# Joining the two Gram jobs of a unit into one job over two PSUM banks, for the last element of a DeltaNet + Mixer kernel

## The chip, the cores and the metric

The kernel runs on one core of a Trainium2 chip. The metric is the device time of one execution in microseconds (us), the median of several runs. The core's engines each work through an own queue in order: PE (TensorE, matmuls; PEld are its weight loads), DVE (VectorE), ACT (ScalarE), POOL (GpSimd), and SP, which only issues DMAs here. SBUF is the working memory, PSUM the memory that matmuls write, in banks of 512 float32 numbers per partition.

## The reference

Two blocks follow one another. The first is a delta rule over 768 steps for 4 batch elements and 8 heads with 48 features each; the second is an MLP-Mixer on the result, seen as 4 x 768 x 384.

```python
k_n = k / (norm(k) + 1e-6)
for t in range(S):                       # per batch element and head
    y[t]  = q[t] @ state
    v_old = k_n[t] @ state
    state = state + beta[t] * outer(k_n[t], v[t] - v_old)
x = y as (B, S, H*D)
u = x + (relu(x^T @ w_tok1) @ w_tok2)^T
out = u + relu(u @ w_ch1) @ w_ch2
```

## The kernel before, in words

The 768 steps of an element are cut into 6 *units* of 128 steps, so there are 24 units, numbered 0 to 23; units 18 to 23 belong to the last element. A unit has two *chunks* of 64 steps (`cc` 0 and 1). Within a chunk the delta rule is solved by matrices: products of all keys with all keys and queries (the *Grams*), the inverse of a triangular matrix made from them, and a short recurrence that takes the state from chunk to chunk.

All work is cut into named jobs, Python generators that issue a few instructions per step. A long text, `order`, says step by step which job goes on; instructions stand on each engine's queue in that order. The jobs that matter here, with the number of the unit (or of the chunk, for `r`) behind the letter:

- `c` and `d` (`grams`, L446): the Grams of chunk 0 and of chunk 1. Four steps, one for each pair of heads, issue two matmuls each (L452); the fifth is one DVE multiplication of the bank with the scaled mask `mb`, into `gm` (L455). Each job holds one of the two PSUM banks of the pool `prep`, which the `j` jobs use too.
- `p` (`prep`): norms and scales of a unit. Steps 1 and 2 are an ACT square (L476) and a DVE sum (L479), step 3 two ACT functions, step 4 a DVE reciprocal and a DVE product (L488, L489), steps 5 and 7 DVE transposes of keys and queries (L369), step 6 makes `mb` on POOL (L511), a buffer that exists once.
- `r` (`recur`): the recurrence of one chunk. Steps 1 to 4 are the matmuls `p_k` (L857), a pair of heads each; step 5 `rest` on DVE (L864); step 6 the matmuls `p_y` and `p_w` (L877, L881); step 7 the copy `w_t` on ACT (L887); step 8 the matmuls `p_s` and `p_y` (L895, L896); step 9 the new state `s_t` on DVE (L904); step 10 the copies of `y` on ACT (L909). Every step needs the one before.
- `j` (`join`): parts of the inverse. Its second step fills both `prep` banks and its third empties them with eight ACT copies (L799, L802).
- `m` (`mixer`): the Mixer of one element, its matmuls 128 rows by 128 columns; it fills the time beside the recurrence of the next element.

The small matmuls use a quarter of TensorE's 128 x 128 array each: rows 0 to 63 or 64 to 127 (the partitions of the operands), and columns 0 to 63 or 64 to 127 (the partitions of the output). Written (rows, columns) with 0 and 1 for the halves, chunk 0's Grams use the quarters (0,0) and (1,1), chunk 1's use (0,1) and (1,0). `p_k` uses (0,0) and (1,1) in a chunk 0 and (0,1) and (1,0) in a chunk 1. Step 6 and step 8 of `r` use all four. The pair of lines that says so for the Grams:

```python
p_g[PAR[i ^ cc], p]        # out: the half i ^ cc of the columns
kqt[f, p, cc]              # in: f is the half i of the rows
```

Of the kernel before, what the change touches and what calls it, by code (L numbers as in the profile page):

```python
# [10 lines left out]
ALU = mybir.AluOpType  # L11
ACTF = mybir.ActivationFunctionType

C = 64
# [9 lines left out]
def kernel(  # L24
# [39 lines left out]
    nc = tc.nc  # L64

    B, H, S, D = q.shape
# [5 lines left out]
    NP = H // 2  # L72
# [22 lines left out]
    def ps_prep(shape, name):  # L95
        return psum.tile(shape, FP32, name=name, tag="prep", bufs=2)
# [36 lines left out]
    TU = 12  # L133
# [15 lines left out]
    for kept, shape in ((kpad, [H, DP]), (qpad, [H, DP]), (kst_of, [NP, 2, D])):  # L149
        for _ in range(NL, NK):  # L150
            n = H * shape[-1]
# [13 lines left out]
    GW = D + 2 * C  # L165
# [20 lines left out]
    PAR = (slice(0, C), slice(C, 2 * C))  # L186
    FEATS = [slice(r.start, r.start + D) for r in PAR]
# [25 lines left out]
    def place(u):  # L213
        return NV + u if u < 2 else (u - 2) % NV

    def before_in(u):
        return max([x for x in range(u) if place(x) == place(u)], default=None)
# [98 lines left out]
    while rounds[-1][-1] < NU - 1:  # L316
        u = rounds[-1][-1] + 1
# [14 lines left out]
    walked = set()  # L332
# [42 lines left out]
    def load_kq(u):  # L375
        b, c = divmod(u, NCH)
        kst = kst_of[slot(u)]
        if u >= TU:
            yield from load_rows(u, 0, k)
            assert last_in(u) in ranked  # L380
            for n, _ in enumerate(stacked(kst, k, u)):
                if n == 3:
                    keys_in.add(u)
                yield
            yield from load_rows(u, 1, q)
            return
        for pad, src in ((kpad, k), (qpad, q)):
            assert last_in(u) is None or (pad is kpad, last_in(u)) in turned
            nc.sync.dma_start(
                out=pad[slot(u)][:, :, 0:D],  # L390
                in_=src[b, :, c * U : (c + 1) * U, :].rearrange("h t d -> t h d"),
            )
            pads_in.add((pad is kpad, u))
            yield
            if src is k and u >= RU:
                for n, _ in enumerate(stacked(kst, k, u)):
                    if n == 3:
                        keys_in.add(u)
                    yield

        heads = kpad[slot(u)].rearrange("t (p par) d -> t p par d", par=2)
        for cc in range(2 if u < RU else 0):
            for par in range(2):
                nc.scalar.copy(kst[PAR[par ^ cc], :, cc], heads[PAR[cc], :, par, 0:D])
                if cc and par:
                    keys_in.add(u)
                yield
# [25 lines left out]
    def blocks(t):  # L433

        if len(t.shape) == 2:
            t = t.rearrange("s (b n) -> s b n", b=NB)
        return t.rearrange("s (p c) n -> s p c n", c=2)

    def gm_of(u):
        return gms[place(u)]  # L440

    grown = set()
    grammed = set()
    made = {}

    def grams(u, cc):  # L446
        kqt = kqts[place(u)]
        p_g = ps_prep([128, NP, 2, C], "p_g")
        for p in range(NP):
            for i in range(2):  # L450
                f = PAR[i] if u < TU else FEATS[i]
                nc.tensor.matmul(p_g[PAR[i ^ cc], p], kqt[f, p, cc, 0], kqt[f, p, cc])  # L452
            yield
        assert before_in(u) is None or 2 * before_in(u) + cc in walked
        nc.vector.tensor_tensor(  # L455
            out=blocks(gm_of(u))[:, :, cc, D:GW].rearrange(
                "s p (two n) -> s p two n", two=2
            ),
            in0=p_g,
            in1=made[u][:, :, cc, None, :].to_broadcast([128, NP, 2, C]), op=ALU.mult,  # L460
        )
        grammed.add((u, cc, False))
        yield

    def prep(u):

# [84 lines left out]
    def z_of(u):  # L551
# [9 lines left out]
        out=low16,  # L561
# [6 lines left out]
        out=even,  # L568
# [5 lines left out]
        out=odd, in0=even, scalar1=-1.0, scalar2=1.0, op0=ALU.mult, op1=ALU.add  # L574
    )
    sides = const.tile([128, 2], FP32, name="sides")
    for i, side in enumerate((even, odd)):
        nc.vector.tensor_tensor(
            out=sides[:, i : i + 1], in0=low16, in1=side, op=ALU.mult
# [25 lines left out]
    def to_parts(u):  # L605
        assert grammed.issuperset([(u, 0, False), (u, 1, False)])
        rnd, j = round_of[u]
        if u < NCH:
            t = turned_of(rnd)
            both = t[:, :, j * NB : j * NB + NB].rearrange("s t b -> s b t")  # L610
            nc.scalar.copy(both, gm_of(u)[:, :, TC.start : TC.start + HB])
            yield
            _, (b1, at1, _), _, (b3, at3, _) = quarters(u)
            nc.vector.tensor_copy(out=t[at1].rearrange("s t b -> s b t"), in_=b1)
            yield
            nc.gpsimd.tensor_copy(out=t[at3].rearrange("s t b -> s b t"), in_=b3)
            masked.add(u)
            yield
            return
        if rnd not in xins:  # L620
            xins[rnd] = dram.tile([RU * 4 * NB, HB, HB], FP32, name="n_dram")
        for i, (block, _, rows) in enumerate(quarters(u)):
            nc.sync.dma_start(out=xins[rnd][rows].rearrange("b s t -> s b t"), in_=block)
            if i == 3:
                masked.add(u)
            yield
# [573 lines left out]
    jobs = {}  # L1200
    for u in range(NU):
        jobs[f"k{u}"] = load_kq(u)
        jobs[f"p{u}"] = prep(u)
        jobs[f"c{u}"], jobs[f"d{u}"] = (grams(u, cc) for cc in range(2))
        jobs[f"t{u}"] = to_parts(u)
        if u < NCH:
            jobs[f"h{u}"] = join_16(u)
        jobs[f"f{u}"] = from_parts(u)
        jobs[f"j{u}"] = join(u)
        jobs[f"v{u}"] = load_v(u)  # L1210
# [64 lines left out]
    s*2 m0 i4 m0*2 i4*2 m0 i4*5 v12*4 m0*2 j13 i4*2 m0 i4 r23 j13 m0 r24 k18*3  # L1275
    r24*3 j13 v13*2 r24 i4 r24*2 p18 i4 p18 m0 i4 p18 m0*2 i4*2 m0 r25*3 p18 r25
    p18*2 r25 m1*3 k18*2 v14 i4 v14 r24 i4*7 k19 m1*3 i4 r25 i4*2 k19*3 v13 k19*2
    v14*2 m1 r25 v13 i4*4 k19 m1 p18 m1 k19 r25*2 p18 m1*2 r26 v13 d18 r26*4 j13
    r25 m1*3 r26*2 c18*2 m1*2 r26*2 k19*4 p19*2 d18*3 c18*2 d18 f14*2 v14 r27*2
    f14*2 r27 p19*2 r27 p19 j14 r27 m1*4 s m1*2 f15*3 m1*2 c18 r26 m1*2 r27*2 j14  # L1280
    j15 j14 r27 f16 m1*3 j15*2 r27 r28*2 k20 p19*2 f16 r27 r28*2 k20*2 f16 j16 m1*4
    r28*3 f15 m1*2 s k20*2 s p19 r28 k20*3 d19 c19 k20 d19 p20 c19 t18 k20 d19*2
    p20 c19 v15 r28 p20 r29 k20*2 m1 p20 r28 c19 r29*3 v15*3 f17*2 r29 m1 p20 k21
    m1*2 c19 k21 r29*2 m1*2 d19 k21 m1*2 p20 m1*2 p20 m1*4 r29*3 m1*2 j16*2 r30
    k21*3 v16 k21*2 v15 k21 r30*4 v16 k21*2 m1 k21 m1*2 c20 r30 d20 c20*3 p21*2 c20
    r30*2 p20 d20 r30 d20*2 p21*2 d20 r31*2 r30 r31*2 t18 r31*3 p21*3 m1*2 r31*2
    c21 d21 c21 d21 c21 d21 v16 m1 v16 c21 v16 r32 d21 r32 d21 m1 t18*2 m1 r32 r31
    t19*2 r32*2 f17 m1 f17 m1*4 t19*2 c21 m1*5 p21 m1*2 f16 t20*3 j17*2 t20 t21*4
    k22 i5 k22*5 j17 k22 m1*2 k22 i5*3 r32 k22 i5*2 m1 i5 m1 r32*3 i5 k22 m1*4
    p22*2 i5 v17 p22 r33*2 k22 r33*3 p22 m1*4 p22 m1 k23 p22 i5 v20 i5*3 m1*2 r32  # L1290
    m1*4 k23 i5 k22 r33 p22 r33 v17 j17 m1*4 r33 i5 m1*6 k23 r33 k23 m1*6 k23 m1*2
    j17 v20 m1 v17*2 k23*2 m1*6 r34*2 d22 v17 k23 r34*3 m1*6 r33 i5*4 m1 r34 p23*2
    c22 d22 c22 d22 c22 d22 i5*2 r34*2 m1 r34 m1 i5*4 m1*4 v20*2 p23 r35*2 k23*3
    c22*2 r35 k23 i5*3 r35 m1*4 i5*3 m1*6 p23 m1*4 d22 t22 r34 i5 m1 p23*2 m1*4
    t22*2 r35*2 m1 f20 p23 m1 r35 m1*2 p23 f21*2 v20 f18 m1*2 v18 m1*3 t22 m1*2
    f18*3 d23 c23 d23 v18 c23 d23 m1 v18 f19*4 c23 d23 m1 c23*2 f20 r35*2 m1*5 d23
    t23*4 m1*2 j18*3 j19 f20 v18 m1 j19 m1*2 j20 i6*2 m1*4 i6*2 v18 j19 r36*5 j20
    r36 i6*2 m2 r36 r37 i6*2 r36 r37*3 m2*3 r37*2 m2 i6*8 v19*2 r37*3 m2 r38 r37
    v19 f20 v19 i6*4 f21 j21 r38 v19 r38*3 m2*3 j20 r38*2 i6*2 j21 r38*2 i6*4 m2*3
    f21 r39 r38 r39*4 m2*7 v21*2 r39*2 m2*4 j21 m2*5 r39*3 m2*2 r40*4 m2 r40*2 j21  # L1300
    i6*2 r40*2 v21 j21 m2*2 i6 v21 m2*2 i6*3 f22*3 r40*2 r41*5 f22 m2*4 r41*2 m2*7
    r41*3 m2 v21 m2*2 r42*2 j22 r42 f23 r42 j22 r42*3 m2*5 f23*2 m2*8 r42*2 j23
    m2*13 p22 m2 v22*3 j22 v22 m2*3 r43 m2 r43*2 r42 r43*2 m2 r43*2 m2*6 r43 m2 j23
    v23 r43*2 r44*4 v22 j23 r44 m2 v23*2 m2*3 r44*2 m2 r44 m2*5 r44 m2*3 r44 m2*3
    v23 r45*5 m2*8 r45 m2*2 r45 f23 j23*2 m2*2 r45*3 m2*6 r46*4 m2*2 v23 r46 m2*9
    r46*2 m2*2 r46*3 m2*7 r47*5 m2*6 r47 m2 r47 m2*2 r47 m2*6 r47 m3*6 m2*5 m3*6
    m2*11 m3*3 m2 m3*159
    """
    for word in order.split():
        name, _, n = word.partition("*")  # L1310
# [34 lines left out]
```

## Time and profile before

| | |
|---|---|
| runs | 638.39, 639.58, 640.07 us; median 639.58 us |
| the profiled execution | 637.11 us, span of its instructions 635.3 us |
| busy in the span | PE 96%, PEld 83%, DVE 70%, ACT 42%, POOL 17% |
| instructions | 21547 |
| granted TensorE clock | 0.981 of full speed on average |
| matmuls of the Grams of units 18 to 23 | first at 283.4 us, last at 385.5 us |

Busy time counts an engine's instructions without overlap. A row of the timeline has the start in us from the start of the span, the time that the row covers, engine, line, operation, tiles (output, then inputs), shapes and the number of records; in brackets stands the time for which the engine was idle before it, and what ended that. A row of a wait table has the total, the number of times, and the longest.

### The profile page before, as it was taken

To read this page: it belongs to the slowest core of one execution; us is meant where nothing else is said; L and a number is where in the kernel's file an instruction comes from. 1 tells how busy PE (TensorE), PEld (TensorE's weight loads), DVE (VectorE), ACT (ScalarE), POOL (GpSimd) and SP (SyncE) were. 2 spreads that over 40 slices of the span, in tenths; PEclk is the share of its full clock that TensorE was granted. 3 is DMA by queue.
4 is the path that set the end of the run, shared out by engine and by line. 5 is a ranking of instruction groups with operands and counts; after the bars stand their busy time and mean duration, and the time that the engine had idled before them with its cause. 6 is when DMAs were issued, how large, how long until landed. Compare 5 with 4: busy or idle time off the path is not lost.

```text
span 635.3 us, 21547 instructions
## 1 busy us (share of the span) xinstructions
PE 607.5 (96%) x9132; PEld 529.5 (83%) x9132; DVE 446.2 (70%) x1132; ACT 268.5 (42%) x693; POOL 108.2 (17%) x146
## 2 busy tenths in 40 slices
PE   8488898999999999999999999999999999999997
PEld 5367786667888888858999999769999977999997
DVE  4988877977899667987969987785627253373643
ACT  7759785447512342226624433145254230223240
POOL 2338354235310221111110010101010000000000
PEclk9979896999999999999999999999999999999999
DMA  9787566666542445154444033201020000000000
GB/s 201 129 148 166 140 134 162 170 135 157 110 115 74 82 118 110 50 125 77 95 101 103 14 95 47 66 11 37 2 54 2 27 1 0 26 1 26 2 26 26
DMA packets 135776, 50.27 MB, mean 79 GB/s; under 512 B 114656, under 2 KB 130144, under 8 KB 135680
## 3 DMA queue, kind: packets, MB, share of 16 engines
q1 hardware_dynamic: 135680, 48.89, 34.9%
q8 instruction: 72, 1.18, 0.8%
q14 instruction: 24, 0.20, 0.1%
HBM read 39.42 MB, written 9.44 MB: 77 GB/s over the span
## 4 chain that ended last, share of the span: by engine, by line
PE 78%; DVE 7%; ACT 5%; SPq 3%; DMA 3%; issue 2%; POOL 1%; ACTq 0%; POOLq 0%; DVEq 0%
PE p_o L1157 25%; PE p_r L1027 18%; PE p_c L1135 8%; PE p_h L1068 5%; PE p L1055 4%; PE p_s L895 3%; PE p_g L452 3%; PE p_k L857 3%; PE p_y L877 2%; DVE x L681 1%; DVE sub L676 1%; PE p_w L881 1%; SPq L413 1%; PE p_ut L1078 1%; DMA d<-in_moe_w_ch_dram 1%
## 5 line engine op out<-in xcount | busy, mean ns | idle before, releaser
L1157 PE MATMUL p_o<-wc,r 128*128 128x192 f32 x720 | 126.8, 330 | 0.6 <-ACT u_t L1082 0.6
L1157 PEld LDWEIGHTS p_o<-wc,r 128*128 128x128 f32 x720 | 116.6, 190 | 2.9 <-ACT u_t L1082 1.1
L1039 DVE TENSOR_TENSOR r<-r,p_r 128x512 f32<-128x512 f32 x90 | 59.7, 684 | 39.7 <-PE p_r L1027 37.2
L1086 DVE TENSOR_TENSOR xb<-xb,p_o 128x192 f32<-128x192 f32 x84 | 29.3, 350 | 58.7 <-PE p_o L1157 58.4
L1036 ACT COPY r<-p_r 128x512 f32<-128x512 f32 x54 | 31.5, 586 | 89.4 <-PE p_r L1027 88.0
L681 DVE TENSOR_TENSOR x<-x,sub 128x84 f32<-128x84 f32 (+24 forms) x178 | 59.8, 336 | 6.1
L676 DVE TENSOR_TENSOR sub<-x 128x84 f32<-128x84 f32 (+24 forms) x178 | 57.4, 322 | 6.7 <-DMA x<-n_dram 2.3
L1135 PE MATMUL p_c<-u_t,wc 128*128 128x256 f32 x216 | 51.1, 387 | 0.2 <-ACT u_t L1082 0.2
L1157 PE MATMUL p_o<-wc,s 128*128 128x192 f32 x288 | 50.1, 329 | 0.3 <-DVE xb L1086 0.3
L426 POOL TENSOR_TENSOR v_st<-v_st,nrm 128x384 f32<-128x384 f32 x24 | 20.3, 845 | 166.7 <-DMA v_st<-in_v_dram 129.1
L1157 PEld LDWEIGHTS p_o<-wc,s 128*128 128x128 f32 x288 | 46.8, 190 | 1.2 <-DVE xb L1086 0.6
L1135 PEld LDWEIGHTS p_c<-u_t,wc 128*128 128x128 f32 x216 | 39.6, 190 | 6.1 <-ACT u_t L1082 0.4
L1043 ACT ACTIVATE r<-r 128x512 f32<-128x512 f32 x54 | 33.8, 630 | 25.0 <-DVE r L1039 24.6
L452 PE MATMUL p_g<-kq 48*64 48x128 f32 (+1 forms) x704 | 38.6, 283 | 3.0 <-ACT kq L524 2.8
L511 POOL TENSOR_TENSOR mb<-mask_c,cs 128x512 f32<-128x512 f32 x20 | 21.4, 1072 | 108.0 <-DVE cs L489 40.9
L909 ACT ACTIVATE xb<-p_y 64x192 f32<-64x192 f32 x96 | 31.2, 325 | 19.6 <-PE p_y L896 12.1
L1027 PE MATMUL p_r<-u_t,wc 128*128 128x128 f32 x288 | 38.5, 277 | 0.0
L1027 PE MATMUL p_r<-t_d,wc 128*128 128x128 f32 x288 | 37.2, 280 | 0.0
L887 ACT COPY w_t<-p_w 128x192 f32<-128x192 f32 x48 | 15.3, 318 | 50.0 <-PE p_w L881 49.3
L1027 PEld LDWEIGHTS p_r<-u_t,wc 128*128 128x128 f32 x288 | 35.3, 192 | 0.3
L1055 PE MATMUL p<-xb,w 128*128 128x384 f32 x96 | 34.9, 511 | 0.0
L452 PEld LDWEIGHTS p_g<-kq 48*64 48x64 f32 (+1 forms) x704 | 28.9, 137 | 7.1 <-ACT kq L524 3.7
(184 smaller groups left out, 1216.0 us busy)
## 6 DMA issues: line engine op xcount, KB each, us to landing
d<-in_moe_w_ch_dram SPq DMA_DIRECT2D x24, 384.0 KB, 4.2
v_st<-in_v_dram SPq DMA_DIRECT2D x96, 48.0 KB, 2.7
out_dram<-xb SPq DMA_DIRECT2D x23, 192.0 KB, 1.9
kst<-in_k_dram SPq DMA_DIRECT2D x64, 48.0 KB, 2.8
n_dram<-gm SPq DMA_DIRECT2D x72, 32.0 KB, 2.0
pads<-in_k_dram SPq DMA_DIRECT2D x24, 96.0 KB, 3.1
pads<-in_q_dram SPq DMA_DIRECT2D x24, 96.0 KB, 2.5
gm<-w_dram SPq DMA_DIRECT2D x72, 32.0 KB, 2.1
```

Source lines behind the costliest of these rows:

```text
L452: nc.tensor.matmul(p_g[PAR[i ^ cc], p], kqt[f, p, cc, 0], kqt[f, p, cc])
L676: nc.vector.tensor_tensor(out=tmp, in0=y[:, :, 0:s, s : s + 1].to_broadcast([n, k, s, w]), in1=y[:, :, s : s + 1, s + 1 : m].to_broadcast( ...
L681: nc.vector.tensor_tensor(out=y[:, :, 0:s, s + 1 : m], in0=y[:, :, 0:s, s + 1 : m], in1=tmp, op=ALU.add,)
L909: nc.scalar.mul(y[:, :, D * i : D * i + D], p_y[PAR[1 - i]], 1.0 if c else -1.0)
L1027: nc.tensor.matmul(p[:, i], pieces[i // width][:, at : at + 128], f[f"u{n}"], start=first and i == 0, stop=True, skip_group_check=True,)
L1036: nc.scalar.copy(o, p)
L1039: nc.vector.tensor_tensor(out=o, in0=o, in1=p, op=ALU.add if sign > 0 else ALU.subtract)
L1043: nc.scalar.activation(o, o, ACTF.Relu)
L1055: nc.tensor.matmul(p_1[dh], piece_of(w1, c, 0)[:, dh * 128 : (dh + 1) * 128], xb[:, c], start=(c == 0), stop=(c == NCH - 1),)
L1068: nc.tensor.matmul(p_h, piece_of(w2, j, c * 128)[:, c * 128 : (c + 1) * 128], r1[j], start=(j == 0), stop=(j == NDH - 1),)
L1135: nc.tensor.matmul(p_c[:, k], piece_of(wc1, cb, f * 128)[:, f * 128 : (f + 1) * 128], u_t[:, cb], start=(cb == 0), stop=(cb == NCB - 1),)
L1157: nc.tensor.matmul(p, a[:, m], wc2[:, m, j], start=(start and i == 0), stop=(i == NM - 1), skip_group_check=True,)
```

## The change

`grams` takes a list of chunks. With one chunk it does what it did. With two it takes both `prep` banks at its first step, and each of its four matmul steps issues the four matmuls of a pair of heads, chunk 0 and chunk 1 in turn: quarters (0,0), (0,1), (1,1), (1,0). Its fifth and sixth steps are the two DVE multiplications, chunk 0 first. Units 0 to 17 keep two jobs; units 18 to 23 have the joint job, named `c`.

```diff
-    def grams(u, cc):
+    def grams(u, chunks):
         kqt = kqts[place(u)]
-        p_g = ps_prep([128, NP, 2, C], "p_g")
+        p_gs = [ps_prep([128, NP, 2, C], "p_g") for _ in chunks]
         for p in range(NP):
             for i in range(2):
-                f = PAR[i] if u < TU else FEATS[i]
-                nc.tensor.matmul(p_g[PAR[i ^ cc], p], kqt[f, p, cc, 0], kqt[f, p, cc])
+                for cc, p_g in zip(chunks, p_gs):
+                    f = PAR[i] if u < TU else FEATS[i]
+                    nc.tensor.matmul(
+                        p_g[PAR[i ^ cc], p], kqt[f, p, cc, 0], kqt[f, p, cc]
+                    )
             yield
-        assert before_in(u) is None or 2 * before_in(u) + cc in walked
-        nc.vector.tensor_tensor(
...
-        grammed.add((u, cc, False))
-        yield
+        for cc, p_g in zip(chunks, p_gs):
+            assert before_in(u) is None or 2 * before_in(u) + cc in walked
+            nc.vector.tensor_tensor(
...
+            grammed.add((u, cc, False))
+            yield
...
-        jobs[f"c{u}"], jobs[f"d{u}"] = (grams(u, cc) for cc in range(2))
+        if u < 18:
+            jobs[f"c{u}"], jobs[f"d{u}"] = (grams(u, [cc]) for cc in range(2))
+        else:
+            jobs[f"c{u}"] = grams(u, [0, 1])
```

In `order` all steps of other jobs keep their sequence. The ten steps of a `c` and `d` become six. Around them, `c20.2` being the second step of the job `c20`, the order is as follows (DMA, SP and Mixer steps that matter little here are left out):

```
unit 18 before: d18.1 r26.2-5 ... r26.6 r26.7 c18.1 c18.2 r26.8 r26.9 ... d18.2-4 c18.3 c18.4 d18.5 ... r27.1-4 ... c18.5
unit 18 after:  r26.2-5 ... r26.6 r26.7 c18.1 r26.8 r26.9 ... c18.2-4 c18.5 ... r27.1-4 ... c18.6
unit 19 before: d19.1 c19.1 d19.2 c19.2 d19.3 d19.4 c19.3 ... r29.1 ... c19.4 r29.2-4 ... c19.5 ... d19.5
unit 19 after:  c19.1 c19.2 c19.3 ... r29.1 ... c19.4 r29.2-4 ... c19.5 ... c19.6
unit 20 before: c20.1 r30.6 d20.1 c20.2-4 p21.1 p21.2 c20.5 r30.7 r30.8 d20.2 r30.9 d20.3 d20.4 p21.3 p21.4 d20.5 r31.1-4 r31.5 r31.6
unit 20 after:  r30.6 c20.1 p21.1 p21.2 r30.7 r30.8 c20.2 r30.9 c20.3 c20.4 c20.5 p21.3 p21.4 c20.6 r31.1-4 r31.5 r31.6
unit 21 before: c21.1 d21.1 c21.2 d21.2 c21.3 d21.3 ... c21.4 r32.1 d21.4 r32.2 d21.5 ... c21.5
unit 21 after:  c21.1 c21.2 c21.3 ... r32.1 c21.4 r32.2 c21.5 ... c21.6
unit 22 before: r34.1 r34.2 d22.1 r34.3 r34.4 ... r34.6 p23.1-2 c22.1 d22.2 c22.2 d22.3 c22.3 d22.4 r34.7 r34.8 ... r35.1 r35.2 c22.4 c22.5 r35.3 r35.4 ... d22.5
unit 22 after:  r34.1-4 ... r34.6 p23.1-2 c22.1-3 r34.7 r34.8 ... r35.1 r35.2 c22.4 c22.5 r35.3 r35.4 ... c22.6
unit 23 before: d23.1 c23.1 d23.2 c23.2 d23.3 ... c23.3 d23.4 ... c23.4 c23.5 r35.8 ... d23.5
unit 23 after:  c23.1 c23.2 ... c23.3 ... c23.4 c23.5 r35.8 ... c23.6
```

More of the change, by code (lines that the diff above doesn't have):

```diff
@@ L444 @@
     made = {}
-    def grams(u, cc):
+    def grams(u, chunks):
         kqt = kqts[place(u)]
-        p_g = ps_prep([128, NP, 2, C], "p_g")
+        p_gs = [ps_prep([128, NP, 2, C], "p_g") for _ in chunks]
         for p in range(NP):
             for i in range(2):
-                f = PAR[i] if u < TU else FEATS[i]
-                nc.tensor.matmul(p_g[PAR[i ^ cc], p], kqt[f, p, cc, 0], kqt[f, p, cc])
-            yield
-        assert before_in(u) is None or 2 * before_in(u) + cc in walked
[L455 to L461, printed above, removed]
-        grammed.add((u, cc, False))
-        yield
+                for cc, p_g in zip(chunks, p_gs):
[3 more added lines that the diff above has]
+                    )
+            yield
+        for cc, p_g in zip(chunks, p_gs):
+            assert before_in(u) is None or 2 * before_in(u) + cc in walked
+            nc.vector.tensor_tensor(
+                out=blocks(gm_of(u))[:, :, cc, D:GW].rearrange(
+                    "s p (two n) -> s p two n", two=2
+                ),
+                in0=p_g,
+                in1=made[u][:, :, cc, None, :].to_broadcast([128, NP, 2, C]),
+                op=ALU.mult,
+            )
+            grammed.add((u, cc, False))
+            yield
     def prep(u):
@@ L1277 @@
     p18*2 r25 m1*3 k18*2 v14 i4 v14 r24 i4*7 k19 m1*3 i4 r25 i4*2 k19*3 v13 k19*2
[L1278 to L1307, printed above, removed]
+    v14*2 m1 r25 v13 i4*4 k19 m1 p18 m1 k19 r25*2 p18 m1*2 r26 v13 r26*4 j13 r25
+    m1*3 r26*2 c18 m1*2 r26*2 k19*4 p19*2 c18*4 f14*2 v14 r27*2 f14*2 r27 p19*2 r27
+    p19 j14 r27 m1*4 s m1*2 f15*3 m1*2 c18 r26 m1*2 r27*2 j14 j15 j14 r27 f16 m1*3
@@ new lines @@
+    j15*2 r27 r28*2 k20 p19*2 f16 r27 r28*2 k20*2 f16 j16 m1*4 r28*3 f15 m1*2 s
+    k20*2 s p19 r28 k20*3 c19 k20 p20 c19 t18 k20 p20 c19 v15 r28 p20 r29 k20*2 m1
+    p20 r28 c19 r29*3 v15*3 f17*2 r29 m1 p20 k21 m1*2 c19 k21 r29*2 m1*2 c19 k21
+    m1*2 p20 m1*2 p20 m1*4 r29*3 m1*2 j16*2 r30 k21*3 v16 k21*2 v15 k21 r30*4 v16
+    k21*2 m1 k21 m1*2 r30 c20 p21*2 r30*2 p20 c20 r30 c20*3 p21*2 c20 r31*2 r30
+    r31*2 t18 r31*3 p21*3 m1*2 r31*2 c21*3 v16 m1 v16*2 r32 c21 r32 c21 m1 t18*2 m1
+    r32 r31 t19*2 r32*2 f17 m1 f17 m1*4 t19*2 c21 m1*5 p21 m1*2 f16 t20*3 j17*2 t20
@@ new lines @@
+    t21*4 k22 i5 k22*5 j17 k22 m1*2 k22 i5*3 r32 k22 i5*2 m1 i5 m1 r32*3 i5 k22
+    m1*4 p22*2 i5 v17 p22 r33*2 k22 r33*3 p22 m1*4 p22 m1 k23 p22 i5 v20 i5*3 m1*2
+    r32 m1*4 k23 i5 k22 r33 p22 r33 v17 j17 m1*4 r33 i5 m1*6 k23 r33 k23 m1*6 k23
+    m1*2 j17 v20 m1 v17*2 k23*2 m1*6 r34*2 v17 k23 r34*3 m1*6 r33 i5*4 m1 r34 p23*2
+    c22*3 i5*2 r34*2 m1 r34 m1 i5*4 m1*4 v20*2 p23 r35*2 k23*3 c22*2 r35 k23 i5*3
+    r35 m1*4 i5*3 m1*6 p23 m1*4 c22 t22 r34 i5 m1 p23*2 m1*4 t22*2 r35*2 m1 f20 p23
@@ new lines @@
+    m1 r35 m1*2 p23 f21*2 v20 f18 m1*2 v18 m1*3 t22 m1*2 f18*3 c23 v18 c23 m1 v18
+    f19*4 c23 m1 c23*2 f20 r35*2 m1*5 c23 t23*4 m1*2 j18*3 j19 f20 v18 m1 j19 m1*2
+    j20 i6*2 m1*4 i6*2 v18 j19 r36*5 j20 r36 i6*2 m2 r36 r37 i6*2 r36 r37*3 m2*3
+    r37*2 m2 i6*8 v19*2 r37*3 m2 r38 r37 v19 f20 v19 i6*4 f21 j21 r38 v19 r38*3
+    m2*3 j20 r38*2 i6*2 j21 r38*2 i6*4 m2*3 f21 r39 r38 r39*4 m2*7 v21*2 r39*2 m2*4
+    j21 m2*5 r39*3 m2*2 r40*4 m2 r40*2 j21 i6*2 r40*2 v21 j21 m2*2 i6 v21 m2*2 i6*3
@@ L1308 @@
+    f22*3 r40*2 r41*5 f22 m2*4 r41*2 m2*7 r41*3 m2 v21 m2*2 r42*2 j22 r42 f23 r42
+    j22 r42*3 m2*5 f23*2 m2*8 r42*2 j23 m2*13 p22 m2 v22*3 j22 v22 m2*3 r43 m2
+    r43*2 r42 r43*2 m2 r43*2 m2*6 r43 m2 j23 v23 r43*2 r44*4 v22 j23 r44 m2 v23*2
+    m2*3 r44*2 m2 r44 m2*5 r44 m2*3 r44 m2*3 v23 r45*5 m2*8 r45 m2*2 r45 f23 j23*2
+    m2*2 r45*3 m2*6 r46*4 m2*2 v23 r46 m2*9 r46*2 m2*2 r46*3 m2*7 r47*5 m2*6 r47 m2
+    r47 m2*2 r47 m2*6 r47 m3*6 m2*5 m3*6 m2*11 m3*3 m2 m3*159
     """
```

## The prediction

> **What bounds the kernel now.** I read the page first, then a table of stretches for the part in which the Grams of units 18 to 23 stand, then the waits of PE there, and then the timeline around each unit, engine by engine. Page, stretch (span, then busy time and records of PE, PEld, DVE, ACT, POOL) and wait:
>
> ```profile
> PE 607.5 (96%) x9132; PEld 529.5 (83%) x9132; DVE 446.2 (70%) x1132; ACT 268.5 (42%) x693; POOL 108.2 (17%) x146
> 280.00:392.00 112.00, 111.24 (x1859) 103.81 (x1859) 96.05 (x238) 46.93 (x119) 15.31 (x23) 1.00 0.38 83
> PE p_g L452 <- ACT gm L802: 0.2, 1, 0.2
> ```
>
> PE is busy in 111.24 of these 112 us. So a Gram matmul saves time if PE's next work then starts earlier, and a wait anywhere in PE's queue that nothing covers is paid in full. Shares do not answer this: overlapping matmuls all count as busy. I go by the start of the next kind of work.
>
> **How the Grams run now.** PE's timeline at units 18, 19 and 21, with the copy `w_t` of unit 18's first chunk (ACT):
>
> ```profile
> 286.62 0.62 PE L452 MATMUL p_g<-kq 48*64 48x128 f32 x8
> 287.80 0.91 PE L452 MATMUL p_g<-kq 48*64 48x128 f32 x20
> 288.47 0.63 PE L857 MATMUL p_k<-s_t,kq 48*64 48x48 f32 x16
> ...
> 301.68 1.13 PE L452 MATMUL p_g<-kq 48*64 48x128 f32 x32
> 302.57 0.62 PE L857 MATMUL p_k<-s_t,kq 48*64 48x48 f32 x16
> ...
> 320.50 1.15 PE L452 MATMUL p_g<-kq 48*64 48x128 f32 x32
> 321.42 0.62 PE L857 MATMUL p_k<-s_t,kq 48*64 48x48 f32 x16
> ```
>
> ```profile
> 286.92 0.32 ACT L887 COPY w_t<-p_w 128x192 f32<-128x192 f32 x1 [0.17 <-PE p_w L881]
> ```
>
> A unit's 16 calls show as 32 records: each call is two passes. Unit 19, where `c` and `d` alternate, takes 302.57 - 301.68 = 0.89 us for 8 passes on each of four quarters, unit 21 321.42 - 320.50 = 0.92: 0.11 us for a pass of four. Unit 18's 20 records take 288.47 - 287.80 = 0.67 us, which is d's 6 passes of 0.11; c's 4 passes run beside them. So the quarters already work side by side, one chunk beside the other, and what counts is the fullest quarter.
>
> **The change part by part.** The same 192 records and 12 DVE multiplications remain; no DMA moves, and on SP and POOL nothing is moved past anything.
>
> *Units 19, 21, 23.* Eight passes on each quarter before and after, in nearly the same places: 0. In 19 and 21 the fourth step now stands inside `p_k`, on the quarters that `p_k` uses; but those carried d's 8 passes ahead of `p_k` already, so the sum on them is unchanged. If breaking up `p_k` is not free, it is two passes, 0.22 us, for each of the two. Bounds 0 to +0.44; I take 0, as the count of passes says.
>
> *Unit 18.* `c18.1` fills the wait for `w_t`, whose copy ends at 286.92 + 0.32 = 287.24, as the old 8 records did. `c18.2-4` are 6 passes, 0.67 us, as the old 20 records. `d18.1`, which goes, stood beside a `p_k` of the other quarters, which is free, as unit 22 shows next. Sum 0, bounds -0.05 to +0.05 (the rounding of these rows).
>
> *Unit 22.* Here is PE at `c22.4`, and farther down a `p_k` with nothing in it:
>
> ```profile
> 369.66 0.26 PE L857 MATMUL p_k<-s_t,kq 48*64 48x48 f32 x2
> 369.69 0.33 PE L452 MATMUL p_g<-kq 48*64 48x128 f32 x2
> ...
> 370.26 0.60 PE L1027 MATMUL p_r<-u_t,wc 128*128 128x128 f32 x3
> ```
>
> ```profile
> 432.11 0.67 PE L857 MATMUL p_k<-s_t,kq 48*64 48x48 f32 x16
> 432.71 0.38 PE L1027 MATMUL p_r<-t_d,wc 128*128 128x128 f32 x1
> ```
>
> With the Gram step 370.26 - 369.66 = 0.60 us, without 432.71 - 432.11 = 0.60 us: the step cost nothing, since chunk 35's `p_k` is on (0,1) and (1,0) and `c22.4` was on the other two. After, `c22.4` brings chunk 1's matmuls too, on just `p_k`'s quarters: two passes of 0.11 that `p_k` must let by, and the 128-row matmuls behind it start 0.22 us later. Bounds 0 (if they slip into gaps of `p_k`) to 0.3; I take +0.22, the count of passes. `d22.1` goes from a place where it was free, and `c22.1-3` fill the same 24 records as before: 0.
>
> *Unit 20* is the one place where a DVE multiplication moves: `c20.5` stood ahead of `r30.9`, and comes now behind it. The timelines of DVE, ACT and PE:
>
> ```profile
> 316.30 0.69 DVE L455 TENSOR_TENSOR gm<-p_g,mb 128x512 f32<-128x512 f32 x1
> 316.91 0.35 DVE L904 TENSOR_TENSOR s_t<-s_t,p_s 128x192 f32<-128x192 f32 x1
> 317.17 0.20 DVE L488 RECIPROCAL ksum<-ksum 128x8 f32<-128x8 f32 x1
> 317.40 0.17 DVE L489 TENSOR_TENSOR cs<-ksum,beta_st 128x8 f32<-128x8 f32 x1
> 317.49 0.68 DVE L455 TENSOR_TENSOR gm<-p_g,mb 128x512 f32<-128x512 f32 x1
> 318.08 0.35 DVE L864 TENSOR_TENSOR rest<-p_k,v_st 128x192 f32<-128x192 f32 x1
> ```
>
> ```profile
> 315.21 0.52 ACT L476 ACTIVATE ksq<-kst 128x384 f32<-128x384 f32 x1
> 315.70 0.32 ACT L887 COPY w_t<-p_w 128x192 f32<-128x192 f32 x1
> ```
>
> ```profile
> 314.69 0.33 PE L452 MATMUL p_g<-kq 48*64 48x128 f32 x2 [0.20 <-ACT gm L802]
> ...
> 316.08 0.25 PE L896 MATMUL p_y<-w_t,gm 64*64 64x48 f32 x1
> ...
> 317.31 0.67 PE L857 MATMUL p_k<-s_t,kq 48*64 48x48 f32 x16
> 318.16 0.31 PE L877 MATMUL p_y<-s_t,kq 48*64 48x48 f32 x2 [0.19 <-issue]
> 318.49 0.25 PE L881 MATMUL p_w<-rest,gm 64*64 64x48 f32 x1
> ```
>
> First the gain that looks sure: PE idles 0.20 us ahead of `c20.1`, whose bank `j16` has not emptied; now `r30.6` goes ahead of it. But the next step, `r30.8`, starts at 316.08 because `w_t` ends at 315.70 + 0.32 = 316.02, and `w_t` starts only when the square `p21.1` (315.21 + 0.52 = 315.73) leaves ACT, which no step here changes. The 0.20 us becomes a wait for `w_t`. Gain 0, bounds -0.20 to 0.
>
> Then the loss. `rest` of chunk 31 is the last thing before `p_w` can start: it ends at 318.08 + 0.35 = 318.43, and `p_w` starts at 318.49. After the change, `c20.5` waits for all of `c20.2-4`, whose six passes stand between `p_s` and `p_k` as d's six did, so DVE starts it when it started `d20.5`: 317.49. From there the queue runs on at its old distances: the reciprocal of `p21.4` follows 318.08 - 317.49 = 0.59 us later, as `rest` did; the multiplication that follows, `c20.6`, starts 317.49 - 317.17 = 0.32 us after the reciprocal; `rest` 0.59 us after that. So `rest` starts at 317.49 + 0.59 + 0.32 + 0.59 = 318.99 instead of 318.08: +0.91 us. `s_t` of `r30.9` may come earlier, but `p_k` stays behind the six passes on its quarters, at 317.31. In PE's queue nothing but `p_k` and two `p_y` stands ahead of `p_w`: the whole 0.91 us is idle PE. Behind `rest` the two transposes of `p21`, which c21 needs, shift as well, by no more than PE itself. POOL's `mb` for unit 21 waits for `c20.6` and comes 0.91 us later, as do its readers. Bounds: 0.59 (if the reciprocal and `cs` hide) to 1.1 (if the pairs no longer overlap, about 0.09 twice more).
>
> Sum: 0 + 0 + 0.22 + 0.91 = +1.13 us; lowest -0.05 + 0 - 0.20 + 0.59 = +0.34, highest 0.44 + 0.05 + 0.3 + 1.1 = +1.9. The profiled execution took 637.11 us and would take 638.24, a factor of 1.0018. It lies 2.47 below the median of the runs shown, so I carry the difference over: 639.58 + 1.13 = 640.7 us.
>
> [...] The changed order puts matmuls of the same rows next to each other: (0,0), (0,1). Today's `p_y` and `p_w`, which read the same rows for different columns, stand so too:
>
> ```profile
> 286.50 0.22 PE L877 MATMUL p_y<-s_t,kq 48*64 48x48 f32 x1
> 286.51 0.22 PE L881 MATMUL p_w<-rest,gm 64*64 64x48 f32 x1
> 286.51 0.22 PE L877 MATMUL p_y<-s_t,kq 48*64 48x48 f32 x1
> 286.52 0.22 PE L881 MATMUL p_w<-rest,gm 64*64 64x48 f32 x1
> 286.56 0.22 PE L877 MATMUL p_y<-s_t,kq 48*64 48x48 f32 x1
> ```
>
> Four start within 0.02 us and the next round 0.06 us after the first, so row neighbours do not wait for each other. [...]
>
> **The rivals.** *Row neighbours take turns* (slower). Then each of the 48 passes of four takes two rounds, 0.11 us more. The two of `c18.1` and the two of `c20.1` are covered by waits for `w_t`; 44 remain, 4.8 us. 639.58 + 1.13 + 4.8 = 645.5 us. It decides from the first joint step on: more than 0.15 us per pass would show it. For it: only that no Gram has been issued in this order. Against it: `p_y` and `p_w`.
>
> *The filled array pays* (faster). Before, unit 18's passes stood as 2 + 4 + 6, unit 20's as 2 + 6 + 6 and unit 22's as 2 + 6 + 2, after as 8 each: 12 passes fewer, 12 x 0.11 = 1.3 us, if none of them was covered and DVE's queue finds slack: 638.3 us. [...] Against it: six of the 12 stand in `p_k` blocks of unchanged length, and the others beside waits for `w_t`.
>
> *Nothing reaches the end*: the later `rest` is made up for in PE's next wait, for `w_t` or the transposes. Then +0.22 remains, 639.8 us. For it: DVE has 112 - 96.05 = 16 us idle in this stretch. Against it: `p_w` follows `rest` within 0.06 us, and PE idles 0.8 us in all of the stretch, too little to take 0.9 up.
>
> **How the numbers follow.** Forecast 0.66, row neighbours 0.10, filled array 0.11, nothing reaches the end 0.13. A measurement of this kernel tells about 0.3% from no change, 1.9 us here. A quarter of the forecast's chance lies beyond it (its highest sum is 1.9, and stalls in a fixed order tend to make others): 0.17, with the row neighbours 0.27 slower. Of the filled array 0.06 beyond 0.3% faster. The rest, 0.67, within. Range: from the low sums less half of the 1.7 us by which the three runs differ (639.8 - 0.8 = 639.0) to the highest sum and as much on top and a little for a second stall (639.58 + 1.9 + 0.8 = 642.3, taken as 642.6); left out are the row neighbours and part of the filled array.
>
> **What would show it.** Right: near 318 us `p_w` of chunk 31 starts some 0.9 us later than `p_k` lets it, with two L455 and the reciprocal between `s_t` and `rest` on DVE; the `p_k` at unit 22 takes 0.82 instead of 0.60 us; 32 records in about 0.9 us at 19, 21 and 23. Wrong: passes of four more than 0.15 us apart; `rest` at its old distance from `p_k`; a new PE wait elsewhere, or PE idle time in 280 to 392 us that does not rise by about 0.9 us.

## The result, and the profile after

The changed kernel takes 641.81 us (median of 20 runs) where the kernel before takes 639.41 us (20 runs beside them). The ratio is 1.0035, with a 95% interval of 1.0019 to 1.0051: that is 2.2 us slower, between 1.2 and 3.3 (the two medians alone differ by 2.4). The prediction was 640.7 us within 639.0 to 642.6. The profiled execution has a span of 642.1 us against 635.3; that is far more than 2.2 us, and the trace tells where it comes from.

The page's busy times, and a stretch over the Grams of units 18 to 23 (span; busy time and records of PE, PEld, DVE, ACT and POOL; clock):

```profile
PE 613.6 (96%) x9132; PEld 534.5 (83%) x9132; DVE 446.5 (70%) x1132; ACT 267.7 (42%) x693; POOL 108.3 (17%) x146
```

```profile
280.00:400.00 120.00, 117.58 (x1876) 108.48 (x1876) 99.41 (x248) 46.68 (x119) 15.34 (x23) 0.97 0.36 79
```

PE's idle time in this stretch is 2.4 us, where it was 0.8, and the granted clock is 0.97, where it was 1.00. The rise of 1.6 us is more than the 0.9 us given as the sign of a right prediction: with the stall come waits for `w_t` that now show as idle, 0.31 us at unit 20 and 0.26 us at unit 18, where the eight matmul records of `c18.1` take 0.41 us instead of 0.62. They are not lost time by themselves, since `w_t` sets the start of what follows either way. PE's waits in 313 to 325 us, and its timeline at chunks 30 and 31:

```profile
PE p_w L886 <- DVE rest L869: 1.3, 1, 1.3
PE p_s L900 <- ACT w_t L892: 0.3, 1, 0.3
```

```profile
318.51 0.25 PE L900 MATMUL p_s<-w_t,gm 64*64 64x48 f32 x1 [0.31 <-ACT w_t L892]
...
321.84 0.25 PE L886 MATMUL p_w<-rest,gm 64*64 64x48 f32 x1 [1.32 <-DVE rest L869]
```

From the start of chunk 30's step 8 (`p_s` and `p_y`, which start together) to chunk 31's `p_w` it was 318.49 - 316.08 = 2.41 us; it is 321.84 - 318.51 = 3.33 us. That is +0.92 us. DVE's timeline shows the cause, the row of instructions that was forecast, two multiplications and the reciprocal between `s_t` and `rest`. `rest` starts 321.44 - 318.51 = 2.93 us after step 8; the prediction had 318.99 - 316.08 = 2.91.

```profile
319.25 0.35 DVE L909 TENSOR_TENSOR s_t<-s_t,p_s 128x192 f32<-128x192 f32 x1 [0.41 <-PE p_y L901]
319.92 0.69 DVE L459 TENSOR_TENSOR gm<-p_g,mb 128x512 f32<-128x512 f32 x1 [0.32 <-PE p_g L453]
320.53 0.19 DVE L493 RECIPROCAL ksum<-ksum 128x8 f32<-128x8 f32 x1
320.75 0.17 DVE L494 TENSOR_TENSOR cs<-ksum,beta_st 128x8 f32<-128x8 f32 x1
320.84 0.69 DVE L459 TENSOR_TENSOR gm<-p_g,mb 128x512 f32<-128x512 f32 x1
321.44 0.35 DVE L869 TENSOR_TENSOR rest<-p_k,v_st 128x192 f32<-128x192 f32 x1
```

PE at unit 22, where all four quarters of `c22.4` now stand inside `p_k`, and at unit 18:

```profile
290.01 0.85 PE L453 MATMUL p_g<-kq 48*64 48x128 f32 x24
290.69 0.63 PE L862 MATMUL p_k<-s_t,kq 48*64 48x48 f32 x16
...
376.16 0.26 PE L862 MATMUL p_k<-s_t,kq 48*64 48x48 f32 x2
...
376.43 0.40 PE L453 MATMUL p_g<-kq 48*64 48x128 f32 x5
376.66 0.38 PE L862 MATMUL p_k<-s_t,kq 48*64 48x48 f32 x8
376.98 0.60 PE L1032 MATMUL p_r<-u_t,wc 128*128 128x128 f32 x3
```

Unit 22's `p_k` takes 376.98 - 376.16 = 0.82 us instead of 0.60. Unit 18's six passes of four take 290.69 - 290.01 = 0.68 us, 0.11 a pass: here too, neighbours of the same rows do not wait for each other.

What was not forecast is the clock. Three stretches of 6 us of the changed kernel, from ahead of the stall on (the number behind POOL's is the granted clock):

```profile
313.00:319.00 6.00, 5.69 (x196) 4.98 (x198) 5.55 (x12) 5.32 (x16) 0.83 (x1) 1.00 0.44 87
319.00:325.00 6.00, 4.68 (x145) 4.29 (x140) 4.91 (x10) 2.92 (x9) 2.72 (x4) 0.87 0.40 74
325.00:331.00 6.00, 6.00 (x52) 5.91 (x44) 3.73 (x15) 0.00 (x0) 0.14 (x1) 0.56 0.30 47
```

In the kernel before, the clock is 1.00 in all of 280 to 392 us. Here it is 0.87 and then 0.56. Since half speed is the only other value in the clock's record of this trace (0.50 in all of 323.45 to 330.28 us), that is 2 x (0.13 + 0.44) x 6 = 6.8 us at half speed, right behind the stall. From `p_w` of chunk 31 to `p_k` of chunk 35 it was 369.66 - 318.49 = 51.17 us and is 376.16 - 321.84 = 54.32: 3.15 us lost. The sum in this execution is 0.92 + 3.15 + 0.22 = 4.3 us behind unit 20's start. The other 2.4 us of the longer span lie ahead of it: 2.2 ahead of 283 us, where both kernels have the same instructions in the same order, and where the changed kernel's record has two more stretches of 3.4 us at half clock (at 74.3 and 115.2 us). So two profiles alone cannot tell the size of a change of 2 us; the steps at known instructions can.

### The profile page after: what moved, and what is told of

It reads as the page before. It is cut to its first block, busy times and chain, and to the rows that moved or that the text cites. A ratio compares the mean times of both kernels' runs of the same rounds, so it can differ in the third digit from the quotient of the medians.

```text
span 642.1 us, 21548 instructions
## 1 busy us (share of the span) xinstructions
PE 613.6 (96%) x9132; PEld 534.5 (83%) x9132; DVE 446.5 (70%) x1132; ACT 267.7 (42%) x693; POOL 108.3 (17%) x146
## 4 chain that ended last, share of the span: by engine, by line
PE 78%; DVE 7%; ACT 5%; DMA 3%; SPq 3%; issue 2%; POOL 1%; DVEq 0%; ACTq 0%; POOLq 0%
PE p_o L1162 25%; PE p_r L1032 19%; PE p_c L1140 6%; PE p L1060 5%; PE p_h L1073 5%; PE p_g L453 3%; PE p_s L900 3%; PE p_k L862 3%; PE p_y L882 2%; PE p_w L886 1%; DVE x L686 1%; PE p_ut L1083 1%; DVE sub L681 1%; SPq L360 1%; PE p_y L901 1%
## 5 line engine op out<-in xcount | busy, mean ns | idle before, releaser
L1162 PE MATMUL p_o<-wc,r 128*128 128x192 f32 x720 | 128.5, 333 | 0.6 <-ACT u_t L1087 0.6
L1162 PEld LDWEIGHTS p_o<-wc,r 128*128 128x128 f32 x720 | 118.3, 193 | 3.0 <-ACT u_t L1087 1.1
L459 DVE TENSOR_TENSOR gm<-p_g,mb 128x512 f32<-128x512 f32 x44 | 29.6, 684 | 8.2 <-PE p_g L453 7.6
```

Of the source, the lines that this page charges most:

```text
L1162: nc.tensor.matmul(p, a[:, m], wc2[:, m, j], start=(start and i == 0), stop=(i == NM - 1), skip_group_check=True,)
```

## The experiments

Two theories stood against each other. The first is the prediction's: in unit 20 the later `c20.5` makes DVE's queue hold `rest` back, which idles PE for 0.9 us; unit 22 adds 0.22 us; to it came, after the result, that PE's idle time brings the clock down in some of the executions. The rival was that the joint order of matmuls costs something in every unit. Each timed run comes with the mean granted clock of its execution. The kernel before was timed 87 times in all beside these experiments; 9 of its executions had a mean clock of 0.975 or less. They come from three occasions: only20, all_but20, dve_moved and stall_filled ran beside 35 of them (4 low), changed_again, rest_first, u20_early and wt_wait_filled beside 23 (0 low), the other three beside 29 (5 low). For the 20 runs of the kernel before that stood beside the first comparison the clock is not on record.

The steps in the traces are summed up here for all of them. Each is worked out as above, as the difference between two starts on PE less the same difference in the kernel before: chunk 30's `p_s` to chunk 31's `p_w`; from there to chunk 35's `p_k`; from there to the next 128-row matmul.

| kernel | unit 20 | on to chunk 35 | unit 22 | clock 0.975 or less | ratio, interval |
|---|---|---|---|---|---|
| changed | +0.92 | +3.15 | +0.22 | 9 of 20 | 1.0035, 1.0019 to 1.0051 |
| changed_again | +0.93 | +4.28 | +0.22 | 2 of 7 | 1.0052, 1.0026 to 1.0078 |
| only20 | +0.93 | +0.01 | 0.00 | 6 of 12 | 1.0020, 0.9996 to 1.0044 |
| all_but20 | 0.00 | +1.06 | +0.22 | 1 of 12 | 0.9990, 0.9971 to 1.0009 |
| dve_moved | +0.50 | 0.00 | +0.01 | 0 of 12 | 0.9994, 0.9976 to 1.0012 |
| stall_filled | +0.92 | +0.04 | +0.22 | 1 of 12 | 1.0039, 1.0018 to 1.0061 |
| stall_filled_small | +0.92 | +0.01 | +0.22 | 0 of 12 | 1.0022, 0.9999 to 1.0045 |
| wt_wait_filled | +0.93 | +0.03 | +0.22 | 1 of 11 | 1.0049, 1.0030 to 1.0068 |
| both_filled | +0.93 | +0.01 | +0.22 | 2 of 13 | 1.0017, 0.9990 to 1.0044 |
| rest_first | +0.36 | +1.39 | +0.21 | 1 of 6 | 1.0058, 1.0036 to 1.0081 |
| u20_early | +0.16 | +0.01 | +0.22 | 2 of 12 | 1.0018, 0.9994 to 1.0042 |
| early20_alone | +0.17 | +1.48 | 0.00 | 3 of 12 | 0.9997, 0.9974 to 1.0019 |

Seven of these traces have the clock at 1.00 behind unit 20 (in all of 313 to 331 us) and 0.00 to 0.04 us in the column after it. The four with 1.4 us or more there (changed, changed_again, rest_first, early20_alone) are those with a stretch at half clock. all_but20 is the exception and comes back below.

### Unit 20 alone, and all but unit 20

Edit of the first: `if u not in (20, ):` in place of `if u < 18:` for the units with two jobs, and in `order` the new steps for unit 20, the old ones for the others. The second has the joint job in the other five units.

> The joint job in unit 20 alone, two jobs in the others. Theory (DVE's queue in unit 20 stalls PE by about 0.9 us, and TensorE's clock then falls to half for some windows in a part of the executions): p_w of chunk 31 about 0.9 us late, ratio to the kernel before 1.001 to 1.003, nearly as much as the whole change. Rival (the joint order of matmuls costs, unit by unit): a sixth of the change, 1.0006 at most.

> The joint job in units 18, 19, 21, 22 and 23, two jobs in unit 20. Theory: only the 0.22 us of unit 22 remain, with perhaps 0.2 us at the join behind unit 18; no half clock near 320 us; ratio 1.0003 to 1.0008. Rival (the joint order costs in every unit): five sixths of the change, 1.003.

Unit 20 alone has the whole stall, and nothing at unit 22. All but unit 20 has no stall, and its 0.22 us at unit 22. So the steps belong to the places that the prediction named, and no cost of a joint job in 18, 19, 21 and 23 shows. The ratio of the second, 0.9990, rules out the rival's 1.003. That of the first, 1.0020, fits the theory, but its interval goes down to 0.9996, so by the time alone it would not be settled. Its executions have the low clock half of the time, the one that was profiled does not. The 1.06 us of all but unit 20, lost in small steps between 338 and 350 us, are not the clock (1.00 in all of that trace from 120 to 638 us); 0.2 of them are a wait of `p_r` for DVE, which no other trace has. I do not know whether they belong to the kernel or to that execution.

### Only the DVE step moved

```diff
-    m1*2 c20 r30 d20 c20*3 p21*2 c20 r30*2 p20 d20 r30 d20*2 p21*2 d20
+    m1*2 c20 r30 d20 c20*3 p21*2 r30*2 p20 d20 r30 d20*2 c20 p21*2 d20
```

> The kernel before, two jobs everywhere; only the DVE multiplication c20.5 is moved to where the change puts it, behind d20.4 and so behind s_t. Theory: the stall of about 0.9 us and the half clock behind it come without any joint job; ratio 1.001 to 1.003, as with the joint job in unit 20 alone. Rival (the joint matmuls do it): 1.000.

The stall comes without a joint job, but at half the size. DVE's timeline of this kernel:

```profile
318.73 0.35 DVE L909 TENSOR_TENSOR s_t<-s_t,p_s 128x192 f32<-128x192 f32 x1 [0.48 <-PE p_y L901]
319.00 0.68 DVE L459 TENSOR_TENSOR gm<-p_g,mb 128x512 f32<-128x512 f32 x1
```

Here the multiplication follows `s_t` at once, 0.27 us behind its start, because its matmuls stand ahead of `p_s` in the order; its row shows no wait for them. In the changed kernel it follows 319.92 - 319.25 = 0.67 us behind, having waited 0.32 us for `p_g`. So of the 0.92 us, 0.50 are DVE's queue, and nearly all of the other 0.42 (0.67 - 0.27 = 0.40) is `c20.5` waiting for matmuls that the joint job issues late. My expectation of the whole 0.9 us missed that difference; the prediction had this wait in its sum. The clock stayed up in all 12 executions, and the ratio, 0.9994, allows for 0.5 us (1.0008) but not for 0.003.

### Filling PE's waits

Matmuls of zeros that nothing reads, in the stall (four of 128x128), in the stall (twelve of 64x64), in the wait for `w_t` (four of 64x64), and in both:

```diff
 stall_filled, stall_filled_small:
-    c20*3 p21*2 c20 r31*2 r30 r31*2 t18 r31*3
+    c20*3 p21*2 c20 r31*2 r30 r31*2 x*4 t18 r31*3
+    c20*3 p21*2 c20 r31*2 r30 r31*2 Y*3 t18 r31*3
 wt_wait_filled (both_filled has this and the Y*3):
-    r30 c20 p21*2 r30*2 p20 c20 r30
+    r30 c20 Y p21*2 r30*2 p20 c20 r30
```

> The changed kernel, with four matmuls of 128x128 zeros by 128 columns (nothing reads them) issued behind p_k of chunk 31, in the stall. They take about 0.25 us each and end before p_w can start. Theory with the clock: the stall of 0.9 us stays, the half clock near 320 us goes; ratio 1.0015 to 1.002 instead of 1.0035. Rival (the half clock comes anywhere by chance and has nothing to do with the stall): the same ratio as the changed kernel, 1.003 to 1.004. If matmuls of zeros do not count as activity for the clock, this run cannot tell.

> The changed kernel with four 64x64 matmuls of zeros (nothing reads them) behind c20.1, in PE's wait for w_t, about 0.45 us, which ends before p_s can start. The stall at rest stays as it is, 0.9 us. [...]

> The changed kernel with twelve 64x64 matmuls of zeros in the stall behind p_k of chunk 31 (about 1.3 us of one quarter pair) instead of four of 128x128. What is open: the first filled kernels had their clock back but not their time, and both traces had a wait of 0.7 to 0.9 us in chunk 37. Theory (that wait was chance, the clock costs time): p_w late by 0.9 us as before, no half clock near 320 us, no wait in chunk 37, ratio 1.001 to 1.0025. Rival (fillers of their own delay something later, or the half clock costs nothing in the end): the wait in chunk 37 again, ratio 1.003 to 1.005.

> The changed kernel with both waits filled, four 64x64 matmuls of zeros behind c20.1 and twelve behind p_k of chunk 31. Theory: the stall of 0.9 us and the 0.2 us of unit 22 remain, the clock is as in the kernel before (at most one run in ten at a mean clock of 0.975 or less), ratio 1.001 to 1.0025. Rival as for the one above: 1.003 to 1.005.

The stall stays in all four, +0.92 or +0.93 us, as expected. The clock comes back with them taken together: 4 of 48 executions at 0.975 or less, against 17 of 39 with the unfilled unit 20 (changed, changed_again, only20) and 9 of 87 before. On the same occasion it is 1 of 12 in stall_filled against 6 of 12 in only20; the two others have no such partner or a weak one. Filling the wait for `w_t` alone, with the 1.3 us at `rest` still there, gave 1 low execution of 11. That points to the shorter wait mattering too, but beside it the unfilled changed_again had only 2 of 7, so it is not shown. Its trace kept the clock:

```profile
319.00:325.00 6.00, 4.69 (x161) 4.22 (x154) 5.34 (x11) 2.83 (x9) 2.67 (x4) 1.00 0.43 82
```

```profile
PE p_w L886 <- DVE rest L869: 1.3, 1, 1.3
```

One trace does not tell, since only20's, with nothing filled, kept it too (1.00 in 313 to 331 us).

The times are not as clean. stall_filled_small (1.0022) and both_filled (1.0017) are where the theory has them without the clock, (0.92 + 0.22) / 639 = 1.0018. The first two, 1.0039 and 1.0049, are as slow as the changed kernel with a good clock. Their traces both had a wait ahead of `p_y` in chunk 38 (the expectations say 37), for which the profile names no releaser and which made the rest 0.7 and 0.9 us later; the two later ones did not have it. I call it neither chance nor an effect of the filling; what slows these two is open.

### The order on DVE, and the place in the wait

```diff
 rest_first:
-    c20*3 p21*2 c20 r31*2 r30 r31*2 t18 r31*3
+    c20*3 p21*2 r31*2 r30 r31*2 t18 r31 c20 r31*2
 u20_early (early20_alone: the same, with two jobs in the other units):
-    r30 c20 p21*2 r30*2 p20 c20 r30 c20*3 p21*2 c20
+    r30 c20 p21*2 r30 c20*4 r30 p20 r30 p21*2 c20
```

> The changed kernel with c20.6 moved on DVE from ahead of rest to behind it. Theory (DVE's queue bounds this place as a whole): p_w of chunk 31 is late by 0.3 instead of 0.9 us, but the two transposes behind c20.6 end as late as before, so the Grams of unit 21, which need them, wait instead and the 0.9 us stay; ratio 1.001 to 1.0035, by the clock. Rival (only the place of rest matters): 0.3 us remain, ratio 1.0005 to 1.001.

> The joint job everywhere; in unit 20 its matmul steps 2 to 4 and its first DVE step stand right behind r30.7, in PE's wait for w_t, instead of behind r30.8 and r30.9. Theory: DVE does the first multiplication while it is idle, ahead of s_t, so rest of chunk 31 is late by 0.1 to 0.4 us instead of 0.9, PE has one long wait less, and no half clock follows near 320 us; ratio 1.000 to 1.001. Rival (joint matmuls cost by themselves): as the changed kernel, 1.003.

> The joint job in unit 20 alone, with its matmul steps 2 to 4 and its first DVE step in the wait for w_t; two jobs in the other units. Theory: the sum of its parts from the traces, +0.16 us in unit 20 and nothing in unit 22; clock as in the kernel before; ratio 0.999 to 1.0015. Rival (a joint job in unit 20 costs wherever it stands): as with the joint job in unit 20 alone, 1.002.

With `rest` ahead of `c20.6`, `p_w` is late by 0.36 us, as expected. Whether the rest of the 0.9 us moves to unit 21 cannot be read from this trace: its clock was at half from 318.7 us on for 3.4 us (0.98 in 313 to 319 us, 0.74 in 319 to 325), and PE shows no wait for the transposes. The time gained nothing: 1.0058, from 6 executions, lies above both forecasts. With the Grams in the wait for `w_t`, unit 20 costs 0.16 us, within the expected 0.1 to 0.4, and its waits are spread:

```profile
PE p_k L862 <- DVE s_t L909: 0.6, 1, 0.6
PE p_w L886 <- DVE rest L869: 0.4, 1, 0.4
```

Of the places tried this one costs the least, but the ratio of u20_early, 1.0018, was forecast as 1.000 to 1.001 and its interval does not settle it; PE still waits twice, and early20_alone had 3.4 us at half clock here in its trace (0.72 in 319 to 325 us), with 1.48 us lost by chunk 35. No version beat the kernel before.

### The changed kernel once more

> The changed kernel once more, for a second trace and more values of the clock. Theory: the stall of 0.9 us at chunk 31 and the 0.2 us at unit 22 in the same places; about half of the executions at a mean clock of 0.975 or less, against one in nine of the kernel before; ratio 1.002 to 1.005. Rival (the low clocks of the first comparison were chance): one in nine, ratio 1.002.

The second trace has the same two steps to 0.01 us, and the clock falls again, earlier and for longer:

```profile
313.00:319.00 6.00, 5.08 (x126) 4.36 (x124) 4.79 (x14) 4.33 (x15) 0.00 (x0) 1.00 0.47 104
319.00:325.00 6.00, 5.05 (x102) 4.63 (x104) 4.25 (x8) 1.93 (x5) 2.86 (x4) 0.52 0.40 64
325.00:331.00 6.00, 6.00 (x42) 5.91 (x35) 3.98 (x14) 0.00 (x0) 0.00 (x0) 0.63 0.08 14
```

Only 2 of its 7 executions are at 0.975 or less, so "about half" is not borne out by this run alone, and its ratio of 1.0052 lies just above the forecast.

## Why the prediction was right, and what it lacked

*Units 18, 19, 21, 23: 0.* Right: no step at any of them that all joint kernels share. From `p_w` of chunk 27 to `p_w` of chunk 28, for example, the traces with a joint job in unit 18 take from 0.01 us less to 0.53 us more than the kernel before, and the three with two jobs there 0.14 to 0.16 us more.

*Unit 22: +0.22.* Right: +0.21 or +0.22 us in every trace with a joint job there, 0.00 or 0.01 in the three without. Counting passes on the fullest quarter was the right measure.

*Unit 20: the 0.20 us ahead of `c20.1` become a wait for `w_t`, gain 0.* Right: the wait for `w_t` is there, 0.31 us, and from chunk 29's `p_w` to chunk 30's step 8 the changed kernel is only 0.06 us faster.

*Unit 20: +0.91.* Right, +0.92 or +0.93 in all seven traces where the steps stand so. The sum over DVE's queue held because each distance came from the same queue and the wait of `c20.5` for its matmuls was counted.

*"The whole 0.91 us is idle PE."* True, and the step that was too short. It priced the idle time at its length; in some executions the idle time was also followed by half the clock. The sum of the prediction, +1.13 us, is half of the measured +2.2 us, and just below its interval; the most likely term that it lacked is the clock. That 641.81 us still lies in the range is in part luck: the room at its top was for larger terms, the spread of the runs and a second stall, not for the clock. The size of the clock's term: the mean granted clock is 0.9761 over the changed kernel's 20 runs and 0.9789 over 87 of the kernel before, so an execution has 2 x 0.0028 x 640 = 3.6 us more at half clock. In the four traces with half clock here, a us of it cost 0.41 to 0.46 us (3.15 for 6.8, 4.28 for 10.2, 1.39 and 1.48 for 3.4), so 3.6 us cost an estimated 1.6. 1.13 + 1.6 = 2.7 us. The recorded times give less: over the 87 executions of the kernel before, compared within each occasion, one with a mean clock 0.01 lower is about 3.3 us longer, which makes 0.9 us of 0.0028 and 2.0 us in all. Both lie within the interval of 1.2 to 3.3, but the clocks compared come from different occasions. The experiments support that the clock depends on unit 20; that it accounts for all the rest in the time is only worked out, since two of the four filled kernels did not get faster.

*The rivals.* Row neighbours do not take turns: 0.11 us a pass. The filled array does not pay: no trace has a gain above 0.1 us at a joint unit. And the stall reaches the end: what a trace has lost by chunk 36 it still has at its end (6.71 and 6.72 us in the changed kernel), but for the wait in chunk 38 of two of them.

*The chances.* I gave 0.67 to within 0.3% and 0.27 to slower; the measured 0.35% is just beyond, its interval on both sides of 0.3%.

## What to carry to other kernels

Small matmuls on separate quarters of the array already ran side by side here where their steps were interleaved, 0.11 us for a pass of four; joining them gained nothing at any of the six units, and lost 0.22 us where the new neighbours shared quarters with work that was waited for. By the count of passes it would gain only where the fullest quarter gets fewer of them ahead of such work; no run here shows such a gain. When an order written out by hand moves one instruction on an engine that is only 86% busy, follow that engine's queue up to the next value that the bottleneck waits for, and count too what the moved instruction itself waits for. And price a stall of TensorE by more than its length: look in several executions at the granted clock behind it. Here it was at half for 6.8 us behind waits of 0.31 and 1.32 us in the changed kernel's trace, and at 1.00 behind waits of the same size in only20's.

## What the hardware showed that I had not expected

The clock fell to half behind waits that are far shorter than the stretch of the fall: 0.31 us and 1.32 us within 3.7 us in the changed kernel, and then 6.8 us at half, from 323.45 to 330.28 us; 0.6 and 1.3 in changed_again, where it fell within the second wait, and then 10.2 us at half. In the traces of the kernel before and of the changed kernel each stretch at half clock that the record shows whole lasts 3.4, 6.8 or 10.2 us. It does not happen in each execution: 17 of 39 were at a mean clock of 0.975 or less.

How much idle time is enough cannot be read from these traces. PE's waits on the way to `p_w` of chunk 31, in order of time, and the clock there and behind:

| trace | PE's waits in 313 to 325 us | clock in 319 to 325 us | clock in 325 to 331 us |
|---|---|---|---|
| changed | 0.3 and 1.3 | 0.87 | 0.56 |
| only20 | 0.3 and 1.3 | 1.00 | 1.00 |
| wt_wait_filled | 0.3 and 1.3 | 1.00 | 1.00 |
| changed_again | 0.6 and 1.3 | 0.52 | 0.63 |
| rest_first | 0.3 and 0.7 | 0.74 | 1.00 |
| early20_alone | 0.6 and 0.4 | 0.72 | 1.00 |
| u20_early | 0.6 and 0.4 | 1.00 | 1.00 |
| dve_moved | 0.2 and 1.0 | 1.00 | 1.00 |

The same waits go with a fall in one trace and with none in another: 0.3 and 1.3 us in the first three, 0.6 and 0.4 in early20_alone and u20_early. Nor does the longer wait tell: 0.7 us in rest_first has a fall, 1.0 us in dve_moved has none, and none of dve_moved's 12 executions had a low clock. What decides in which executions the clock falls, no run here shows.
